# Attention scores on four TensorE tiles, products on two, and block means of v by TensorE, in a kernel of banded attention and two feed-forward networks

## Chip, cores, metric

One NeuronCore of a Trainium2 chip. The metric is the device time of one execution in microseconds (us), as the median of several runs. The engines are PE (TensorE, matmuls, with its weight loads PEld), DVE (VectorE), ACT (ScalarE), POOL (GpSimd) and SP (SyncE, whose queue, SPq, issues all loads and stores here).

## What is computed

Two batches, 8 heads, 768 positions, head size 64. Each query sees the keys less than 16 positions away, and beside them one summary for each block of 32 positions: the maximum of the block's keys and the mean of its values. The result, as 1536 tokens by 512, goes through two feed-forward networks (FFN) with 2048 hidden units.

```python
# attention; block = 32, window = 16
k_sum = k.reshape(B, H, nb, block, D).max(axis=3)
v_sum = v.reshape(B, H, nb, block, D).mean(axis=3)
scores_l = scale * np.matmul(q, k.transpose(0, 1, 3, 2))
mask_l = np.abs(pos[:, None] - pos[None, :]) < window
scores_s = scale * np.einsum('bhsd,bhnd->bhsn', q, k_sum) + np.log(block)
scores_all = np.concatenate([np.where(mask_l, scores_l, -1e9), scores_s], axis=-1)
a = softmax(scores_all)
x = np.matmul(a, np.concatenate([v, v_sum], axis=2))
# then, on x as [tokens, 512]:
h = x @ w_in;  x = (h - np.tanh(h)) @ w_out
h = x @ w_in2; out = (h * np.tanh(softplus(h))) @ w_out2
```

## The kernel before

**Units.** The attention is done in 12 units u, two batches of six windows of 128 queries. Heads are taken in 4 pairs (hp), e = 0 or 1 is the head of a pair, and s = 0 or 1 the half of 64 queries in a window. For each half there are 120 keys: 24 summaries of blocks and 96 keys of the band. The host lays out q and k transposed (the two heads of a pair on partitions 0 to 63 and 64 to 127), v by windows (`vw`), and v transposed once more (`vt`) for its block sums.

**Scores** (`qk`). The q of a u lies in a tile `qz` twice, once for each e, with zeros on the other head's 64 partitions, so that the product over all 128 partitions gives one head's scores. A score has 128 rows of weights and 64 output columns (a column tile for each s); 16 of them make one e.

**Softmax and products.** `softmax` takes mask, maximum and exponential of one e (VectorE, L330, then four ScalarE activations, L335), `norm` divides, `a_trans` transposes (TensorE, L355) and copies to `asb`, and `av` multiplies with v (L369): 16 products for one e, all on the column tile of that e. `x_hi` and `x_lo` split the result into two parts that the FFNs multiply apart.

**Summaries.** `k_sum` (VectorE, L264) takes the block maxima of k of a u, `k_fill` copies those of a whole batch beside the band of each u. `v_sum` adds up the loaded `vtc` (VectorE, or GpSimd by halving adds), `v_trans` turns the sums by TensorE (L294) and copies them, scaled by 1/32, into the v tile `vu[0]`; `v_fill` copies them from there by DMA into the two other v tiles (L303). The three v tiles are reused by the u that follow.

**Order.** The schedule is written by hand: each engine works through its instructions in the order of the program. Ahead of the loop stand the loads of the first batch's own k, of q for u = 0 to 2, one v and three vt. Then step j makes the scores of (u, e) = (j // 2, j % 2), the softmax of the step before, the normalisation three steps back, the transposes five steps back and the products six steps back; the table `todo` adds loads, sums and fills at chosen steps, and its loads go to SP's queue in that order. Between the steps stands the conversion of the FFN's weights (L114 to L137), and at the end of the loop the first steps of the FFN, whose 96 steps follow.

Of the kernel before, what the change touches and what calls it, by code (L numbers as in the profile page):

```python
# [26 lines left out]
def kernel(  # L27
# [17 lines left out]
    nc = tc.nc  # L45
# [133 lines left out]
    def attention(actx):  # L179
# [7 lines left out]
        qz = [kq.tile([128, 2, HP, 128], F32, name=f"qz{n}") for n in range(3)]  # L187
        vu = [con.tile([KA, 2, H, D], F32, name=f"vu{n}") for n in range(3)]
# [4 lines left out]

        def q_zero(n):
            for e in range(2):
                other = qz[n][64 * (1 - e):64 * (1 - e) + 64, e]
                if n < 2:
                    nc.vector.memset(other, 0.0)
                else:
                    nc.scalar.copy(other, qz[0][64 * (1 - e):64 * (1 - e) + 64, e])  # L200

        def constants():
# [20 lines left out]
            k_edges(UPB)  # L223
            tops = top_tiles(2)

        vtc, ksum, vsum = {}, {}, {}
# [20 lines left out]
        def load_q(u):  # L247
            for e in range(2):
                nc.sync.dma_start(out=qz[u % 3][64 * e:64 * e + 64, e], in_=qt_d[u, 64 * e:64 * e + 64])

        def load_v(u):
            for s in range(2):
                nc.sync.dma_start(out=vu[u % 3][WND[s][0]:WND[s][1], s], in_=vw_d[u, s])

        def load_vt(b, g):
            vtc[b, g] = two.tile([128, HP, 256], F32, tag="vtc", name="vtc", bufs=3)
            nc.sync.dma_start(out=vtc[b, g], in_=vt_d[b, g])
# [16 lines left out]
        def v_sum(b, g, part, pool=False):  # L274
            if b not in vsum:
                vsum[b] = two.tile([128, HP, NB], F32, tag="vsum", name="vsum")
            t = vtc[b, g].rearrange("p a (n c) -> p a n c", c=BLK)
            o = vsum[b][:, :, g * 8:(g + 1) * 8]
            t, o = (z[:, 2 * part:2 * part + 2] for z in (t, o))
            if not pool:  # L280
                nc.vector.tensor_reduce(out=o, in_=t, axis=AX.X, op=ALU.add)
                return
            c = BLK // 2
            while c > 1:
                nc.gpsimd.tensor_tensor(
                    out=t[:, :, :, 0:c], in0=t[:, :, :, 0:c], in1=t[:, :, :, c:2 * c], op=ALU.add
                )
                c //= 2
            nc.gpsimd.tensor_tensor(out=o, in0=t[:, :, :, 0], in1=t[:, :, :, 1], op=ALU.add)

        def v_trans(b):
            p = pst("tr")
            for hp in range(HP):
                nc.tensor.transpose(p[0:NB, hp * 128:(hp + 1) * 128], vsum[b][:, hp, :], ident)  # L294
# [6 lines left out]
        def v_fill(n):  # L301
            for s in range(2):
                nc.sync.dma_start(  # L303
                    out=vu[n][SUM[s][0]:SUM[s][1], s], in_=vu[0][SUM[s][0]:SUM[s][1], s]
                )
# [3 lines left out]
        def qk(u, e):  # L309
            p = pst(("s", "tr")[e])  # L310
            pv = p[:, 0:HP * KA].rearrange("p (a n) -> p a n", a=HP)
            for hp in range(HP):
                for s in range(2):
                    k0 = s * (NB + T)
                    nc.tensor.matmul(
                        out=pv[T * s:T * s + T, hp, :],
                        lhsT=qz[u % 3][:, e, hp, T * s:T * s + T],
                        rhs=kt[u % NK][:, hp, k0:k0 + KA],
                    )
            sc[u, e] = pv  # L320
# [43 lines left out]
        def av(u, e):  # L364
            if e == 0:
                xps[u] = pst("x").rearrange("p (a n) -> p a n", a=HP)
            for hp in range(HP):
                for s in range(2):
                    nc.tensor.matmul(  # L369
                        out=xps[u][64 * e:64 * e + 64, hp, T * s:T * s + T],  # L370
                        lhsT=vu[u % 3][:, s, 2 * hp + e, :],
                        rhs=asb[u, e][:, hp, T * s:T * s + T],
                    )
# [27 lines left out]
        for n in range(3):  # L401
            q_zero(n)
# [8 lines left out]
        for u in range(UPB):  # L411
            if u == 0:
                v_sum(0, 0, 1, True)
# [4 lines left out]
        at(1, L(load_v, 1))  # L418
        at(2, L(load_v, 2), L(v_sum, 0, 0, 0))
        at(3, L(load_k, 6), L(load_k, 7), L(v_sum, 0, 1, 1))  # L420
        at(4, L(load_k, 8), L(v_sum, 0, 1, 0), L(v_sum, 0, 2, 0), L(v_sum, 0, 2, 1, True))
        before_av[5] = L(v_trans, 0)
        at(5, L(v_fill, 1), L(v_fill, 2), L(load_k, 9), L(load_k, 10))
# [3 lines left out]
        at(8, L(k_sum, 9), L(load_vt, 1, 0))  # L427
# [338 lines left out]
```

## Time and profile before

| | us |
|---|---|
| runs of the kernel before (3) | 611.49 to 612.99, median 611.64 |
| the profiled execution | 611.33, of which 609.6 span |
| busy: PE, DVE, ACT, POOL | 594.0, 421.1, 330.2, 53.2 |
| first FFN matmul, and the FFN step from which PE no longer stops | 73.46, 94.27 |

A profile shows one execution. Its times count from the start of the span; the 1.7 us between the span and the execution's time lie around it. An engine's idle time is given in square brackets in a timeline, with what ended it. Names such as `s`, `tr`, `aT` and `x` are the four kinds of PSUM tile, each in two copies: the scores of e = 0 are in `s`, those of e = 1 in `tr`, transposes in `aT`, products in `x`; the FFNs use all four.

### The profile page before, as it was taken

How to read it: one execution, taken by the hardware profiler on the slowest of the kernel's cores; microseconds unless marked ns; L12 is line 12 of the kernel's file. 1: busy time of each engine (PE TensorE's matmuls, PEld its weight loads, DVE VectorE, ACT ScalarE, POOL GpSimd, SP SyncE). 2: the span in 40 equal slices, each digit the busy share in tenths (PEclk: the TensorE clock that was granted, in tenths of full speed). 3: DMA queues.
4: the chain of work that ended last, by engine and by line, in shares of the span. 5: the costliest groups of instructions: out<-in, count | busy, mean ns of one | idle time of the engine just before them, and what ended most of it. 6: DMA issues, size and time to landing. Idle time of an engine off the chain costs nothing.

```text
span 609.6 us, 9228 instructions
## 1 busy us (share of the span) xinstructions
PE 594.0 (97%) x3212; PEld 494.0 (81%) x3212; DVE 421.1 (69%) x972; ACT 330.2 (54%) x793; POOL 53.2 (9%) x109
## 2 busy tenths in 40 slices
PE   7698999999999999999999999999999999999997
PEld 6577888888888888888888888888888888888886
DVE  6668967887342222367777579997768777598785
ACT  5678958887242222356776446664454444454442
POOL 5446652000000000000000000000000000000000
PEclk9899999999999999999999999999999999999999
DMA  9999547766121000125662101100010000100001
GB/s 239 232 254 261 162 134 230 230 216 198 45 54 33 1 0 1 34 83 160 198 195 74 52 1 52 53 19 1 1 69 1 1 1 0 70 1 1 1 1 69
DMA packets 32302, 52.20 MB, mean 86 GB/s; under 512 B 3392, under 2 KB 25920, under 8 KB 32256
## 3 DMA queue, kind: packets, MB, share of 16 engines
q1 hardware_dynamic: 32256, 51.62, 29.3%
q8 instruction: 25, 0.41, 0.3%
q14 instruction: 21, 0.17, 0.1%
HBM read 48.07 MB, written 3.15 MB: 84 GB/s over the span
## 4 chain that ended last, share of the span: by engine, by line
PE 90%; DMA 7%; SPq 1%; DVE 1%; POOL 0%; ACT 0%; issue 0%; POOLq 0%
PE s L486 7%; PE aT L486 7%; PE s L487 7%; PE aT L487 7%; PE s L488 7%; PE tr L487 7%; PE x L487 7%; PE aT L488 7%; PE tr L488 7%; PE x L488 7%; PE tr L486 7%; PE x L486 7%; DMA qz<-in_qt_dram 3%; DMA kt<-in_kw_dram 2%; PE x L369 2%; PE aT L355 1%
## 5 line engine op out<-in xcount | busy, mean ns | idle before, releaser
L511 DVE TENSOR_TENSOR glo<-t,ghi 128x512 fp32r<-128x512 f32 x48 | 33.4, 696 | 86.9 <-ACT ghi L506 86.9
L506 ACT ACTIVATE ghi<-t 128x512 fp32r<-128x512 f32 x48 | 30.2, 629 | 97.3 <-PE tr L488 97.3
L486 PE MATMUL s<-xhi,w 128*128 128x512 f32 x192 | 74.9, 390 | 0.0
L486 PE MATMUL aT<-xhi,w 128*128 128x512 f32 x192 | 74.9, 390 | 0.0
L487 PE MATMUL s<-xlo,w 128*128 128x512 f32 x192 | 74.7, 389 | 0.0
L488 PE MATMUL s<-xhi,w 128*128 128x512 f32 x192 | 74.7, 389 | 0.0
L487 PE MATMUL aT<-xlo,w 128*128 128x512 f32 x192 | 74.7, 389 | 0.0
L488 PE MATMUL aT<-xhi,w 128*128 128x512 f32 x192 | 74.7, 389 | 0.0
L114 ACT ACTIVATE top<-raw 128x256 f16<-128x256 bf16 x128 | 61.5, 486 | 12.3 <-ACT w L132 5.3
L121 DVE SCALAR_TENSOR_TENSOR cv<-raw,top 128x256 int32<-128x256 int32 x128 | 55.5, 435 | 11.3 <-ACT top L114 7.7
L132 ACT ACTIVATE w<-cv 128x256 fp32r<-128x256 f32 x120 | 47.6, 402 | 10.7 <-DVE cv L121 9.7
L137 DVE TENSOR_TENSOR w<-cv,w 128x256 fp32r<-128x256 f32 x114 | 48.4, 426 | 0.1
L542 DVE SCALAR_TENSOR_TENSOR t<-n,r 128x512 f32<-128x512 f32 x48 | 33.1, 689 | 17.5 <-ACT r L539 17.3
L335 ACT ACTIVATE aa<-aa,neg 128x120 f32<-128x120 f32 x96 | 36.6, 383 | 15.0 <-DVE neg L330 15.0
L511 DVE TENSOR_TENSOR glo<-n,ghi 128x512 fp32r<-128x512 f32 x48 | 33.1, 690 | 15.3 <-ACT ghi L506 15.3
L506 ACT ACTIVATE ghi<-n 128x512 fp32r<-128x512 f32 x48 | 30.3, 631 | 24.3 <-PE tr L487 16.1
L486 PEld LDWEIGHTS s<-xhi,w 128*128 128x128 f32 x192 | 36.0, 188 | 7.6
L486 PEld LDWEIGHTS aT<-xhi,w 128*128 128x128 f32 x192 | 36.0, 188 | 7.6
L488 PEld LDWEIGHTS s<-xhi,w 128*128 128x128 f32 x192 | 36.1, 188 | 7.5
L488 PEld LDWEIGHTS aT<-xhi,w 128*128 128x128 f32 x192 | 36.1, 188 | 7.5
L487 PEld LDWEIGHTS s<-xlo,w 128*128 128x128 f32 x192 | 36.0, 188 | 7.4
L487 PEld LDWEIGHTS aT<-xlo,w 128*128 128x128 f32 x192 | 36.0, 188 | 7.4
(99 smaller groups left out, 1307.6 us busy)
## 6 DMA issues: line engine op xcount, KB each, us to landing
raw<-in_w_dram SPq DMA_DIRECT2D x128, 255.8 KB, 3.6
vu<-in_vw_dram SPq DMA_DIRECT2D x24, 192.0 KB, 6.0
qz<-in_qt_dram SPq DMA_DIRECT2D x24, 128.0 KB, 6.9
vtc<-in_vt_dram SPq DMA_DIRECT2D x6, 512.0 KB, 6.8
out_dram<-o SPq DMA_DIRECT2D x9, 256.0 KB, 2.1
kt<-in_kw_dram SPq DMA_DIRECT2D x6, 320.0 KB, 6.4
kt<-in_kw_dram SPq DMA_DIRECT2D x6, 256.0 KB, 4.3
out_dram<-t SPq DMA_DIRECT2D x3, 256.0 KB, 2.1
```

The lines of the kernel that those rows point to most:

```text
L114: nc.scalar.activation(out=tops[n % len(tops)].bitcast(F16).rearrange("p (n t) -> p n t", t=2)[:, :, 1], in_=raws[n].bitcast(BF16).rearran ...
L121: nc.vector.scalar_tensor_tensor(out=tmps[n], in0=raws.pop(n).bitcast(I32).rearrange("p (n t) -> p n t", t=2)[:, :, 0], scalar=13, in1=top ...
L132: nc.scalar.activation(out=hi, in_=t, func=ACTF.Copy)
L137: (nc.gpsimd if on_pool else nc.vector).tensor_tensor(out=W[i][:, 1, o:o + PW], in0=tmps.pop(n).bitcast(F32), in1=W[i][:, 0, o:o + PW].bit ...
L335: nc.scalar.activation(out=aa[u][:, e, hp, :], in_=aa[u][:, e, hp, :], func=ACTF.Exp, scale=-1.0, bias=neg[u][:, e, hp:hp + 1], accum_out= ...
L369: nc.tensor.matmul(out=xps[u][64 * e:64 * e + 64, hp, T * s:T * s + T], lhsT=vu[u % 3][:, s, 2 * hp + e, :], rhs=asb[u, e][:, hp, T * s:T ...
L486: nc.tensor.matmul(out=out, lhsT=w[0], rhs=x[0], start=first, stop=False)
L487: nc.tensor.matmul(out=out, lhsT=w[0], rhs=x[1], start=False, stop=False)
L488: nc.tensor.matmul(out=out, lhsT=w[1], rhs=x[0], start=False, stop=last)
L506: nc.scalar.activation(out=ghi, in_=t, func=ACTF.Copy)
L511: nc.vector.tensor_tensor(out=glo, in0=t, in1=ghi.bitcast(F32), op=ALU.subtract)
L542: nc.vector.scalar_tensor_tensor(out=ts[z], in0=ns[z], scalar=2.0, in1=rs[z], op0=ALU.add, op1=ALU.mult)
```

## The change

It does three things.

1. **Scores.** q is loaded once into a tile `qt`, by one DMA in place of two, without zeros. A score uses the 64 partitions of its head as weights' rows. The scores of both e of a u are made at the even step, e in the innermost loop, so that the instructions go round four tiles of 64 x 64.
2. **Products.** `av` makes both e of a u at the odd step, again e innermost, so that the instructions go round two column tiles.
3. **Means of v.** The loads of `vt`, `v_sum` and `v_trans` go. There are seven v tiles instead of three, and all six of the first batch are loaded ahead of the loop. GpSimd writes zeros into the summary rows of the v tiles and builds two constants: `means`, which holds 1/32 at a block's rows, and `fold`, four identities of 24 stacked. At step 4 (and 17 for the second batch) `v_part` multiplies the six v with `means` in 12 products over four column tiles of 32, and ScalarE copies the result to `vp`; at step 5 (18) `v_fold` adds up the four parts and two ScalarE copies write the means into the batch's first v tile; ten DMAs per batch, not four, then fill the other five.

```diff
-        qz = [kq.tile([128, 2, HP, 128], F32, name=f"qz{n}") for n in range(3)]
-        vu = [con.tile([KA, 2, H, D], F32, name=f"vu{n}") for n in range(3)]
+        qt = [kq.tile([128, HP, 128], F32, name=f"qt{n}") for n in range(3)]
+        NV = UPB + 1
+        vu = [con.tile([KA, 2, H, D], F32, name=f"vu{n}") for n in range(NV)]
+        ZC = 4 * (UPB - 1)
+        means = [con.tile([KA, ZC + 32], F32, name=f"means{s}") for s in range(2)]
+        fold = con.tile([128, NB], F32, name="fold")
...
+            for n in range(NV):
+                for s in range(2):
+                    nc.gpsimd.memset(vu[n][SUM[s][0]:SUM[s][1], s], 0.0)
+            for s in range(2):
+                nc.gpsimd.memset(means[s], 0.0)
...
+        def v_part(b):
+            p = pst("aT")
+            for k in range(UPB // 2):
+                for t in range(4):
+                    w, s = 2 * k + t // 2, t % 2
+                    nc.tensor.matmul(
+                        out=p[32 * t:32 * t + 32, :],
+                        lhsT=means[s][:, ZC - 4 * w:ZC - 4 * w + 32],
+                        rhs=vu[(b * UPB + w) % NV][:, s].rearrange("p h d -> p (h d)"),
+                        start=k == 0, stop=k == UPB // 2 - 1,
+                    )
+            vpart[b] = two.tile([128, H * D], F32, tag="vp", name="vp", bufs=1)
+            nc.scalar.activation(out=vpart[b], in_=p, func=ACTF.Copy)
+
+        def v_fold(b):
+            p = pst("aT")
+            nc.tensor.matmul(out=p[0:NB, :], lhsT=fold, rhs=vpart[b])
+            n = b * UPB % NV
             for s in range(2):
                 nc.scalar.activation(
-                    out=vu[0][SUM[s][0]:SUM[s][1], s].rearrange("p h d -> p (h d)"), in_=p[0:NB, :],
-                    func=ACTF.Copy, scale=1.0 / BLK,
+                    out=vu[n][SUM[s][0]:SUM[s][1], s].rearrange("p h d -> p (h d)"), in_=p[0:NB, :],
+                    func=ACTF.Copy,
                 )
...
-        def qk(u, e):
+        def qk(u):
...
             for hp in range(HP):
                 for s in range(2):
-                    k0 = s * (NB + T)
-                    nc.tensor.matmul(
-                        out=pv[T * s:T * s + T, hp, :],
-                        lhsT=qz[u % 3][:, e, hp, T * s:T * s + T],
-                        rhs=kt[u % NK][:, hp, k0:k0 + KA],
-                    )
+                    for e in range(2):
+                        d = slice(64 * e, 64 * e + 64)
+                        k0 = s * (NB + T)
+                        nc.tensor.matmul(
+                            out=sc[u, e][T * s:T * s + T, hp, :],
+                            lhsT=qt[u % 3][d, hp, T * s:T * s + T],
+                            rhs=kt[u % NK][d, hp, k0:k0 + KA],
+                        )
...
         load_q(0)
-        load_vt(0, 0)
+        load_v(0)
+        load_v(1)
         load_q(1)
-        load_v(0)
-        load_vt(0, 1)
+        for u in range(2, UPB):
+            load_v(u)
         load_q(2)
-        load_vt(0, 2)
...
-            at(2 * u + 1, L(load_v, u))
...
+        for u in range(UPB + 1, NU):
+            at(2 * u - 7, L(load_v, u))
...
-        before_av[5] = L(v_trans, 0)
-        at(5, L(v_fill, 1), L(v_fill, 2), L(load_k, 9), L(load_k, 10))
+        before_av[4] = L(v_part, 0)
+        before_av[5] = L(v_fold, 0)
+        at(5, *[L(v_fill, u) for u in range(1, UPB)])
+        at(5, L(load_k, 9), L(load_k, 10), L(load_v, 6))
```

On SP's queue, around the fills of the first batch (numbers in names are those of the tiles: `kt_90`, `kt_91` and `kt_92` hold k of u = 9, 10 and 11 here, `vu_100` is the first v tile), there stands before:

```order
L249 DMA qz_99<-in_qt_dram 64x512 x2
L303 DMA vu_101<-vu_100 24x512 x2
L303 DMA vu_102<-vu_100 24x512 x2
L229 DMA kt_90<-in_kw_dram 128x4x160
L229 DMA kt_91<-in_kw_dram 128x4x160
L253 DMA vu_100<-in_vw_dram 96x512 x2
L249 DMA qz_97<-in_qt_dram 64x512 x2
L229 DMA kt_92<-in_kw_dram 128x4x160
```

Three fills more, two DMAs each, now stand ahead of the k loads of u = 9 and 10, and one v load more ahead of that of u = 11.

On the same queue at the same place after the change:

```order
L263 DMA qt_99<-in_qt_dram 128x512
L313 DMA vu_101<-vu_100 24x512 x2
L313 DMA vu_102<-vu_100 24x512 x2
L313 DMA vu_103<-vu_100 24x512 x2
L313 DMA vu_104<-vu_100 24x512 x2
L313 DMA vu_105<-vu_100 24x512 x2
L244 DMA kt_90<-in_kw_dram 128x4x160
L244 DMA kt_91<-in_kw_dram 128x4x160
L267 DMA vu_106<-in_vw_dram 96x512 x2
L263 DMA qt_97<-in_qt_dram 128x512
L267 DMA vu_100<-in_vw_dram 96x512 x2
L244 DMA kt_92<-in_kw_dram 128x4x160
```

The k loads kept their order among themselves and moved behind the fills as a block.

On TensorE, from the end of the scores of u = 2 (`kt_91`) to the start of those of u = 3 (`kt_92`), there stands before:

```order
L315 MATMUL tr<-kt_91,qz_99 64x120 x8
L355 MATMUL aT<-ident,aa 120x128 x4
L294 MATMUL tr<-ident,vsum 24x128 x4
L315 MATMUL s<-kt_92,qz_97 64x120 x8
```

The four transposes of the sums of v stood between the transposes of a and the next scores.

On TensorE at the same place after the change (a row is one product here, of two instructions; the eight means before the first row read alike):

```order
L291 MATMUL aT<-vu_104,means_107 32x512
L291 MATMUL aT<-vu_104,means_108 32x512
L291 MATMUL aT<-vu_105,means_107 32x512
L291 MATMUL aT<-vu_105,means_108 32x512
L368 MATMUL aT<-ident,aa 120x128 x4
L302 MATMUL aT<-vp,fold 24x512
L329 MATMUL s<-kt_92,qt_97 64x120
L329 MATMUL tr<-kt_92,qt_97 64x120
```

The means stand between the scores of u = 2 and the first transposes of a, the fold behind these, and scores of both e follow in turn.

## Rows read from the trace of the kernel before

**Rows 1.** The page's part 2, busy tenths in 40 slices of the span.

```profile
PE   7698999999999999999999999999999999999997
...
DMA  9999547766121000125662101100010000100001
```

**Rows 2.** Windows by stage: us, busy of PE, PEld, DVE, ACT, POOL, PEclk, DMA, GB/s.

```profile
10.30:17.10 6.80, 3.97 (x65) 3.61 (x66) 5.56 (x37) 4.65 (x24) 4.16 (x10) 1.00 1.06 274
...
40.30:58.43 18.13, 15.69 (x224) 13.35 (x222) 17.61 (x88) 15.43 (x65) 12.57 (x22) 1.00 1.03 257
58.43:73.46 15.03, 15.03 (x216) 12.99 (x217) 13.36 (x64) 13.23 (x58) 7.66 (x13) 1.00 0.59 167
73.46:94.27 20.81, 20.81 (x166) 17.14 (x165) 13.60 (x33) 14.54 (x39) 13.04 (x18) 1.00 0.52 150
```

**Rows 3.** VectorE's timeline: start, us, instruction, idle time before it and its releaser.

```profile
33.74 0.69 DVE L264 TENSOR_REDUCE ksum<-kt 128x16 f32<-128x512 f32 x1 [2.96 <-DMA kt<-in_kw_dram]
...
39.21 0.69 DVE L264 TENSOR_REDUCE ksum<-kt 128x16 f32<-128x512 f32 x1 [1.69 <-DMA kt<-in_kw_dram]
```

**Rows 4.** The page's part 6, DMA issues: count, KB each, us to landing.

```profile
vu<-in_vw_dram SPq DMA_DIRECT2D x24, 192.0 KB, 6.0
qz<-in_qt_dram SPq DMA_DIRECT2D x24, 128.0 KB, 6.9
vtc<-in_vt_dram SPq DMA_DIRECT2D x6, 512.0 KB, 6.8
out_dram<-o SPq DMA_DIRECT2D x9, 256.0 KB, 2.1
kt<-in_kw_dram SPq DMA_DIRECT2D x6, 320.0 KB, 6.4
kt<-in_kw_dram SPq DMA_DIRECT2D x6, 256.0 KB, 4.3
```

**Rows 5.** Windows around the third q, columns as in Rows 2.

```profile
15.00:17.07 2.07, 0.01 (x1) 0.04 (x1) 1.63 (x4) 1.65 (x10) 1.52 (x2) 1.00 1.03 259
...
17.77:21.18 3.41, 3.41 (x30) 2.92 (x25) 2.74 (x15) 2.41 (x15) 1.74 (x4) 0.50 1.04 239
```

**Rows 6.** TensorE's timeline, scores (L315) and half products (L369).

```profile
17.07 1.22 PE L315 MATMUL s<-kt,qz 128*64 128x120 f32 x15 [2.53 <-DMA qz<-in_qt_dram]
...
65.81 0.32 PE L315 MATMUL tr<-kt,qz 128*64 128x120 f32 x1
...
65.92 0.99 PE L315 MATMUL tr<-kt,qz 128*64 128x120 f32 x15
...
72.39 1.15 PE L369 MATMUL x<-asb,vu 120*64 120x64 f32 x16
...
86.32 1.15 PE L369 MATMUL x<-asb,vu 120*64 120x64 f32 x16
```

**Rows 7.** ScalarE from 41.00 to 66.30: busy, mean ns, idle before and releaser.

```profile
L335 ACT ACTIVATE aa<-aa,neg 128x120 f32<-128x120 f32 x40 | 15.2, 383 | 3.4 <-DVE neg L330 3.4
...
L377 ACT ACTIVATE xhi<-x 128x512 fp32r<-128x512 f32 x5 | 2.9, 586 | 0.2 <-PE x L369 0.2
```

**Rows 8.** SP's queue, issues by start and us.

```profile
24.44 3.88 SPq L303 DMA_DIRECT2D vu<-vu  x4
28.42 1.51 SPq L229 DMA_DIRECT2D kt<-in_kw_dram  x2
...
40.35 0.79 SPq L253 DMA_DIRECT2D vu<-in_vw_dram  x2
```

**Rows 9.** Line L303, the fills of v: ns min/median/max of an issue.

```profile
L303 SPq DMA_DIRECT2D vu<-vu x8: 714/748/1192, 24.4 to 62.8; - x8
```

**Rows 10.** VectorE's copy that feeds the products at 72.39.

```profile
70.36 0.68 DVE L359 COPY asb<-aT 120x512 f32<-120x512 f32 x1
```

**Rows 11.** GpSimd's timeline: last constants, and weights' low parts.

```profile
7.62 0.57 POOL L98 MEMSET top<- 128x256 int32 x2
...
91.58 2.56 POOL L137 TENSOR_TENSOR w<-cv,w 128x256 fp32r<-128x256 f32 x3 [1.42 <-ACT w L132]
```

More of the change, by code (lines that the diff above doesn't have):

```diff
@@ L192, in attention @@
         WND = ((NB, KA), (0, KW))
[L194 to L200, printed above, removed]
         def constants():
@@ L223, in constants @@
             k_edges(UPB)
+            for n in range(NV):
[3 more added lines that the diff above has]
+                nc.gpsimd.memset(means[s], 0.0)
+                cols = means[s][:, ZC + 2 * s:ZC + 2 * s + 2]
+                nc.gpsimd.memset(cols, 1.0 / BLK)
+                own = WND[s][0] + WIN
+                for pattern, base, mul in (([[-BLK, 2]], -own, 1), ([[BLK, 2]], own + BLK - 1, -1)):
+                    nc.gpsimd.affine_select(
+                        out=cols, in_=cols, pattern=pattern, base=base, channel_multiplier=mul,
+                        compare_op=ALU.is_ge, fill=0.0,
+                    )
+            nc.gpsimd.tensor_tensor(out=fold, in0=ident[:, 0:NB], in1=ident[:, 32:32 + NB], op=ALU.add)
+            for t in (2, 3):
+                nc.gpsimd.tensor_tensor(out=fold, in0=fold, in1=ident[:, 32 * t:32 * t + NB], op=ALU.add)
             tops = top_tiles(2)
-        vtc, ksum, vsum = {}, {}, {}
+        ksum, vpart = {}, {}
         def load_k(u):
@@ L247, in load_q @@
         def load_q(u):
-            for e in range(2):
-                nc.sync.dma_start(out=qz[u % 3][64 * e:64 * e + 64, e], in_=qt_d[u, 64 * e:64 * e + 64])
+            nc.sync.dma_start(out=qt[u % 3], in_=qt_d[u])
         def load_v(u):
             for s in range(2):
[L253 to L257, printed above, removed]
+                nc.sync.dma_start(out=vu[u % NV][WND[s][0]:WND[s][1], s], in_=vw_d[u, s])
         def k_sum(u):
@@ L272, in k_fill @@
                 eng.tensor_copy(kt[u % NK][:, :, o:o + NB], ksum[u // UPB])
[L274 to L286, printed above, removed]
-                )
-                c //= 2
-            nc.gpsimd.tensor_tensor(out=o, in0=t[:, :, :, 0], in1=t[:, :, :, 1], op=ALU.add)
@@ L312, in qk @@
             for hp in range(HP):
                 for s in range(2):
[L314 to L320 removed]
+                    for e in range(2):
+                        d = slice(64 * e, 64 * e + 64)
[4 more added lines that the diff above has]
+                            rhs=kt[u % NK][d, hp, k0:k0 + KA],
+                        )
@@ L362, in a_trans, with av @@
             asb[u, e] = t
-        def av(u, e):
-            if e == 0:
-                xps[u] = pst("x").rearrange("p (a n) -> p a n", a=HP)
+        def av(u):
+            xps[u] = pst("x").rearrange("p (a n) -> p a n", a=HP)
             for hp in range(HP):
                 for s in range(2):
[L369 to L373, printed above, removed]
+                    for e in range(2):
+                        nc.tensor.matmul(
+                            out=xps[u][64 * e:64 * e + 64, hp, T * s:T * s + T],
+                            lhsT=vu[u % NV][:, s, 2 * hp + e, :],
+                            rhs=asb[u, e][:, hp, T * s:T * s + T],
+                        )
         def x_hi(u):
@@ L426, in attention @@
         at(7, L(k_sum, 8), L(load_k, 11))
-        at(8, L(k_sum, 9), L(load_vt, 1, 0))
-        at(9, L(k_sum, 10), L(load_vt, 1, 1))
+        at(8, L(k_sum, 9))
+        at(9, L(k_sum, 10))
         at(10, L(k_sum, 11), L(k_fill, 6))
-        at(11, L(load_vt, 1, 2), L(v_sum, 1, 0, 0))
-        at(12, L(v_sum, 1, 0, 1, True), L(conv_ahead, n_raw))
-        at(13, L(v_sum, 1, 1, 0))
-        at(14, L(v_sum, 1, 1, 1, True))
-        at(15, L(v_sum, 1, 2, 0, True))
-        at(16, L(v_sum, 1, 2, 1))
-        before_av[17] = L(v_trans, 1)
-        at(17, L(v_fill, 1), L(v_fill, 2))
+        at(15, L(conv_ahead, n_raw))
+        before_av[17] = L(v_part, 1)
+        before_av[18] = L(v_fold, 1)
+        at(18, *[L(v_fill, u) for u in range(7, NU)])
         for u in range(7, 12):
@@ L455, in attention @@
                 x_hi(xu)
-            if j < NJ:
-                qk(j // 2, j % 2)
+            if j < NJ and j % 2 == 0:
+                qk(j // 2)
             nu, nr = divmod(j - 3, 2)
@@ L470, in attention @@
                 before_av[j]()
-            if LA <= j < NJ + LA:
-                av(*divmod(j - LA, 2))
+            if LA <= j < NJ + LA and (j - LA) % 2:
+                av((j - LA) // 2)
             for f in todo.get(j, []):
```

22 lines of the change are left out of this document (6 added, 16 removed).

## Prediction

> **What bounds the kernel now.** I read the page's slices first. TensorE is at 9 in every slice of 15.2 us but the first, the second, the fourth and the last, and the DMA engines are at 9 in just the first four [rows 1]. So there is a front of some 60 to 90 us in which TensorE waits, and behind it a stretch in which TensorE is the bound. The windows by stage say the same [rows 2]: from 58.43 us on PE is busy for the whole of each window, before that it is not. Only the front is touched by the change, so the sum is that of a shift: how much earlier or later does TensorE come to the step that starts at 94.27, from which on it never pauses.
>
> What holds the front is then read from VectorE's timeline [rows 3]. Two of its idle stretches, of 2.96 and 1.69 us, end at a block maximum of k (L264) that waits for a load of k: those of u = 9 and u = 11, at 33.74 and 39.21. The engine works in order, so all softmaxes queued behind stand too. After that VectorE (17.61 of 18.13 us) and ScalarE (15.43) are nearly full up to 58.43 [rows 2].
>
> **What the change does, part by part.**
>
> *Loads before the third q.* Before, q of u = 2 is issued behind six own k loads, two q, two vt and one v; after, behind six k, two q and all six v of the first batch. With the sizes of the page, two issues to a q or a v [rows 4]: up to and with it 6 x 256 + 3 x 256 + 2 x 512 + 384 = 3712 KB before, 6 x 256 + 3 x 256 + 6 x 384 = 4608 KB after. The 896 KB more (0.92 MB) are 3.5 us at the 259 GB/s of that stretch [rows 5]. The scores of u = 2 waited for this q until 17.07 [rows 6]; so they start at 20.6. Over the whole front 3 MB of vt loads go, which helps only where a load ends a wait.
>
> *Scores on four tiles.* Fifteen scores in a row take 0.99 us, one alone 0.32: one starts each (0.99 - 0.32) / 14 = 0.05 us. A half of the products, 16 instructions, takes 1.07 (from 72.39 to the window's end at 73.46), 0.067 each [rows 2, 6]. A score moves 120 columns, a product 64. That the scores are no slower means that their two column tiles already run at once; the products of a half, all on one tile, do not. On four tiles the 32 scores of a u should take 8 x 0.10 = 0.8 us, not 1.6; at half clock, twice that. TensorE stood from before 15.00 until 17.07 and was granted 0.50, its lower level of 1.2 GHz, from 17.77 to 21.18, 4.1 us after its restart [rows 5]. It will stand longer after the change, so I let it run at half clock from 20.6 to 24.7: scores of u = 2 done at 22.3.
>
> *Means on TensorE.* Twelve products of 512 columns, 24 instructions, on four column tiles, 6 each. By 120 columns in 0.10 us, 512 take 0.43: 2.6 us, doubled until 24.7. That makes 2.8 of the 6 passes by 24.7, 1.4 us for the rest and 0.2 to drain: 26.3. ScalarE copies the result (0.59, as the 512-column copy of x in [rows 7]), then does the four exponentials of u = 2 that are queued behind (4 x 0.38), then the first copy of the folded means: 29.0. The fold, 512 columns once, lies beside the exponentials.
>
> *Fills on SP's queue.* Before, four copies of the means into two other v tiles start at 24.44, and the k load of u = 9 is issued behind them at 28.42 [rows 8]. After, there are ten, from 29.0 on. One keeps the queue for 0.748 us in the median [rows 9], about 0.80 with the step to the next: 8.0 us. The load of u = 9 is issued at 37.1, 8.7 later than before. Up to and with k of u = 11 there follow 320 x 3 + 384 x 2 + 256 = 1984 KB (2.03 MB), 7.9 us at 257 GB/s [rows 2], and a start of 1.1 (the 2.1 us of 256 KB out, less its 1.0 at that rate [rows 4]). k of u = 11 lands at 46.1, not 39.21: **+6.9**.
>
> *What is made good behind it.* From 41.00 to 66.30 ScalarE is idle for 3.4 us before exponentials and 0.2 before copies of x [rows 7], while VectorE is nearly full. Three sums of v go from VectorE there, of as many elements as a maximum of k, 0.69 each [rows 3], 2.1 in all; the added copy of the means takes 0.6 of ScalarE. So between 2.1 - 0.6 = 1.5 and 3.6 - 0.6 = 3.0; I take 2.5, as the two then wait for each other less: **-2.5**. From 58.43 to 73.46 VectorE (13.36 of 15.03) and ScalarE (13.23) stay nearly full [rows 2] with the same work as before. TensorE's faster products gain there only its own delay: the copy that feeds the products at 72.39 [rows 6] starts at 70.36 and takes 0.68 [rows 10], so TensorE comes to it 1.35 late: **-1.3**.
>
> *Tail.* From 73.46 on TensorE is the bound, with four half products among its work up to and with 86.32 [rows 6]. Four halves at 1.07 become two whole ones that should take no more each than one half: 2.1 us less, of which I count **-2.0**, since two tiles end a little after one. The last half gains nothing: the first layer at 94.27 needs weights whose low parts GpSimd ends at 94.14 [rows 11], a chain that does not pass through the products.
>
> *At no gain or cost.* The memsets of q go, where VectorE waits for k anyway, and GpSimd's sums of v. Fourteen memsets of 24 x 512 come on GpSimd, 0.57 each by the two of 128 x 256 that take 0.57 [rows 11], 8.0 us; with some 2.3 for the other constants GpSimd comes to its fills of k at about 18.5, before the q of 20.6. Without that cover each us of delay would cost one. The means of the second batch fall where TensorE has idle time.
>
> **Sum.** +6.9 - 2.5 - 1.3 - 2.0 = +1.1 us on the profiled execution's 611.33 us (span 609.6): 612.4. The median of the runs, 611.64, is 0.3 above that execution: 612.7.
>
> **A rule against the products' gain.** The scores of before load weights of all 128 rows on either column tile and still start each 0.05 us [rows 6]: a tile's weights come in while the other tile works. The Trainium skill, TensorE: Matmul & The Clock Gate, Part 3, says that weight loads overlap with running products only where their row groups differ; the new products use the same rows on both tiles. By that rule the 2.0 would be lost; this trace speaks against it.
>
> **Rivals.**
> 1. *The relief of the loads reaches the end (faster).* If ten copies on an otherwise empty queue cost what two v loads do, 0.79 for the pair [rows 8], they take 4.0 us, not 8.0, and k of u = 11 is 4.0 earlier: 608.7. For it: 3 MB less to load, so that queues are emptier. Against: eight such copies, none under 0.714 [rows 9].
> 2. *The four column tiles of the means run one after the other (slower).* 24 x 0.43 = 10.3 us, not 2.6, in the first batch, all ahead of the fills: +7.7, 620.4. It decides as soon as a pass of four takes over 0.6 us. The trace shows two tiles at once, never four.
> 3. *TensorE stays at half clock (slower).* It stands twice for 6 us and more. If the means run wholly at 0.50, they take 5.2 us, not 3.9: +1.3. If, after the wait for k of u = 9, a u at twice its time (0.8 of scores, 1.1 of products, about as much of transposes by my estimate, so twice 3 us) exceeds the pitch at which VectorE feeds it (13.36 us for about three u's in [rows 2], 4.5 each), each of three u's adds up to 1.5, most of it hidden by that pitch's own gaps: 615.
> 4. *The change does not do there what it says: the products on two tiles don't overlap.* The 2.0 us are lost: 614.7.
>
> **How the numbers follow.** The forecast 0.39, rival 1 0.32, rival 2 0.07, rival 3 0.12, rival 4 0.10. About 0.3% (1.8 us) is what a measurement of this kernel can tell from no change. Low end: rival 1 with 3.0 made good (-0.5), loads at the 274 GB/s of [rows 2] (-0.5) and a tail of 3 (-1.0): 606.7. High end: rival 4 with 1.5 made good (+1.0) and part of rival 3: 617. Rival 2 is left outside, with a little at both ends. Within 0.3% lie most of the forecast's spread (609.8 to 613.5) and the near edge of rival 1: 0.38. Faster 0.34, slower 0.28. The likeliest time is 612.7.
>
> **What would show each step.** In the profile of the changed kernel: the scores of u = 2 start at 20 to 21 us behind a q load; the means end near 26; ten copies stand on SP from 29 to 37; VectorE is idle for several us before the maximum of u = 9 and again before that of u = 11 at about 46; ScalarE and VectorE are then full to about 75; the first FFN step starts at 75 to 77, the last pause ends at 95. I am wrong if VectorE doesn't wait there, if the copies take half the time, or if a whole set of products takes the 2.1 us of two halves.

## The result, and the profile after

The changed kernel takes 617.48 us in the median of five runs (616.25 to 618.95), beside 612.68 (five runs) for the kernel before: a ratio of 1.0082, 95% interval 1.0058 to 1.0105. It is slower by 0.8%. The forecast was 612.7, in a range of 606.7 to 617.0, with a chance of 0.28 for slower; the time lies 0.5 us above the range. The profiled execution took 616.25 us (span 614.5), 4.9 more than that of before.

Part 2 of the page of the changed kernel, against [rows 1]:

```profile
PE   5657989999999999999999999999999999999997
...
PEclk8687999999999999999999999999999999999999
DMA  9655556776302000034663101100010000100001
```

TensorE is at 9 from the seventh slice on, not from the fifth, and the DMA engines, which were at 9 in the first four slices, are there in the first alone. So loads are fewer, as meant, but they no longer fill the time. ScalarE's and SP's timelines, and then VectorE's, say what they wait for:

```profile
27.33 0.60 ACT L298 ACTIVATE vp<-aT 128x512 f32<-128x512 f32 x1 [6.85 <-PE aT L291]
```

```profile
29.96 8.40 SPq L313 DMA_DIRECT2D vu<-vu  x10
38.46 1.30 SPq L244 DMA_DIRECT2D kt<-in_kw_dram  x2
...
42.38 0.55 SPq L244 DMA_DIRECT2D kt<-in_kw_dram  x1
```

```profile
41.93 0.69 DVE L274 TENSOR_REDUCE ksum<-kt 128x16 f32<-128x512 f32 x1 [7.38 <-DMA kt<-in_kw_dram]
...
47.60 0.69 DVE L274 TENSOR_REDUCE ksum<-kt 128x16 f32<-128x512 f32 x1 [1.91 <-DMA kt<-in_kw_dram]
...
63.22 0.69 DVE L372 COPY asb<-aT 120x512 f32<-120x512 f32 x1 [1.74 <-PE aT L368]
```

ScalarE waits 6.85 us for the means. The ten fills keep SP's queue from 29.96 to 38.4, where four began at 24.44 [rows 8]; k of u = 9 is issued at 38.46, not 28.42. VectorE's wait for it grew from 2.96 [rows 3] to 7.38 us. The third row is a wait that the kernel before did not have in this place; it is taken up below.

TensorE's timeline, with the scores of u = 2 (21.06), the means, the products of u = 5 (66.68), the scores of u = 9 (67.76) and the first FFN step:

```profile
21.06 0.43 PE L329 MATMUL s<-kt,qt 64*64 64x120 f32 x1 [4.53 <-DMA qt<-in_qt_dram]
...
23.10 4.07 PE L291 MATMUL aT<-vu,means 120*32 120x512 f32 x24
...
66.68 1.15 PE L382 MATMUL x<-asb,vu 120*64 120x64 f32 x32
67.76 0.31 PE L329 MATMUL s<-kt,qt 64*64 64x120 f32 x1
...
68.74 0.65 PE L368 MATMUL aT<-ident,aa 128*120 128x128 f32 x4
...
81.72 0.50 PE L492 MATMUL s<-xhi,w 128*128 128x512 f32 x1
```

A product is two instructions here, and the 16 for one e that are spoken of ahead of the prediction are instructions of eight products. A whole set of products, 32 instructions, takes 1.08 us (66.68 to 67.76), as long as 16 did before, and the 32 instructions of the scores of a u take 0.98 (67.76 to 68.74), where 16 had taken about that [rows 6]. Both parts do on TensorE what the change says.

To see where the time goes, the same instruction is found in two traces by its place among its kind on its engine (the maximum of k of u = 9 is the tenth), and the two starts are subtracted. In us against the kernel before, one profiled execution of each kernel, with the experiments that are told below (E1 to E14 for short):

| start of | before | after | E1 | E3 | E4 | E5 | E11 | E14 |
|---|---|---|---|---|---|---|---|---|
| VectorE, first softmax | 11.68 | +0.0 | +1.7 | -0.5 | +0.8 | +0.1 | +0.1 | -0.3 |
| softmax u = 2, e = 0 | 19.70 | +3.5 | +5.6 | -0.8 | +3.9 | +1.8 | +1.6 | -1.0 |
| maximum of k, u = 9 | 33.74 | +8.2 | +3.1 | -4.1 | +9.2 | -0.4 | -0.4 | -3.8 |
| maximum of k, u = 11 | 39.21 | +8.4 | +3.1 | -4.7 | +10.7 | -0.3 | -0.5 | -4.2 |
| softmax u = 7, e = 1 | 53.49 | +7.1 | +1.8 | -5.4 | +9.4 | -1.5 | -1.2 | -3.4 |
| softmax u = 8, e = 0 | 55.49 | +8.3 | +1.6 | -4.2 | +9.0 | -1.7 | -1.2 | -3.4 |
| softmax u = 9, e = 1 | 64.45 | +9.6 | +2.8 | -4.1 | +13.0 | -0.5 | -1.7 | -3.3 |
| last store's issue (its end) | 606.88 | +5.1 | -1.6 | -8.5 | +13.7 | -4.9 | -6.1 | -4.6 |

Three things stand in the column of after: 8.4 us are lost up to the maximum of u = 11, 1.15 more up to the softmax of u = 9, and 4.4 come back between there and the end. The first row shows how far two executions differ of themselves: the changed kernel and E1 are the same up to there and lie 1.7 us apart, which the other rows carry along.

### The profile page after: what moved, and what is told of

The parts are those of the page before. It is cut to its first block, busy times and chain, and to the rows that moved or that the text cites. A ratio compares the mean times of both kernels' runs of the same rounds, so it can differ in the third digit from the quotient of the medians.

```text
span 614.5 us, 9299 instructions
## 1 busy us (share of the span) xinstructions
PE 585.2 (95%) x3256; PEld 479.5 (78%) x3256; DVE 415.7 (68%) x961; ACT 329.9 (54%) x793; POOL 52.3 (9%) x109
## 4 chain that ended last, share of the span: by engine, by line
PE 90%; DMA 3%; ACT 2%; DVE 2%; SPq 1%; issue 1%; POOL 0%; POOLq 0%
PE s L492 7%; PE aT L492 7%; PE s L494 7%; PE aT L493 7%; PE s L493 7%; PE tr L493 7%; PE x L493 7%; PE aT L494 7%; PE tr L494 7%; PE x L494 7%; PE tr L492 7%; PE x L492 7%; PE x L382 2%; ACT aa L348 1%; DMA kt<-in_kw_dram 1%; PE aT L368 1%
## 5 line engine op out<-in xcount | busy, mean ns | idle before, releaser
L121 DVE SCALAR_TENSOR_TENSOR cv<-raw,top 128x256 int32<-128x256 int32 x128 | 55.4, 434 | 10.7 <-ACT top L114 6.9
L132 ACT ACTIVATE w<-cv 128x256 fp32r<-128x256 f32 x120 | 47.5, 402 | 10.0 <-DVE cv L121 9.0
L512 ACT ACTIVATE ghi<-n 128x512 fp32r<-128x512 f32 x48 | 30.3, 632 | 24.4 <-PE tr L493 16.1
```

The costliest lines, as they stand in the source:

```text
L121: nc.vector.scalar_tensor_tensor(out=tmps[n], in0=raws.pop(n).bitcast(I32).rearrange("p (n t) -> p n t", t=2)[:, :, 0], scalar=13, in1=top ...
L132: nc.scalar.activation(out=hi, in_=t, func=ACTF.Copy)
L512: nc.scalar.activation(out=ghi, in_=t, func=ACTF.Copy)
```

## Experiments

### The two halves of the change, each alone

E3, the kernel before with the new scores and products:

```diff
-                        lhsT=qz[u % 3][:, e, hp, T * s:T * s + T],
-                        rhs=kt[u % NK][:, hp, k0:k0 + KA],
+                            lhsT=qt[u % 3][d, hp, T * s:T * s + T],
+                            rhs=kt[u % NK][d, hp, k0:k0 + KA],
...
-            if LA <= j < NJ + LA:
-                av(*divmod(j - LA, 2))
+            if LA <= j < NJ + LA and (j - LA) % 2:
+                av((j - LA) // 2)
```

> The kernel before with the new scores and the new products alone; vt, sums of v, three v tiles and four fills stay. Theory 1 (the products bring what the tail showed, the loss is all in the means): 606.5 to 608.5, 3 to 4.5 us faster than before. Theory 2 (a TensorE that finishes sooner stands longer and is granted the lower clock, which eats the gain): 610.5 or more.

601.60 us against 611.44, ratio 0.9859 (0.9822 to 0.9897): 9.8 us faster, by far more than either theory gave. It is also faster than both kernels of this study.

E4, the changed kernel with `qz`, `qk` and `av` of before put back:

> The changed kernel with the scores and products of before (q twice with zeros, one e at a time); the means by TensorE, seven v tiles and ten fills stay. Theory 1: the k waits are as in the changed kernel, and without the products' gain the end is at 619 to 622. Theory 2 (the means cost little, scores and products lose the time): 611 to 613.

625.96 against 611.44, ratio 1.0263 (1.0218 to 1.0308): 14.5 us slower, again more than expected. The two medians' differences, -9.8 and +14.5, make +4.7; the change itself measured +4.8. So what is slow is the means, and scores and products pay for two thirds of it.

Where E3's gain arises is told by the two parts of it apart. E11 takes over `av` alone, E14 `qk` and the load of q alone:

> The kernel before with the new products alone; scores, q and the means are those of before. Theory 1 (the 10 us that scores and products bring together come from two places: 4.4 us in the tail from the products, 4 to 5 us before 40 us from the scores and the one DMA for q): nothing changes before 40 us, the tail brings 4.0 to 4.8 us, the end is at 607. Theory 2 (the products bring the early gain too): 602 to 604.

607.26 against 611.32, ratio 0.9938 (0.9906 to 0.9970).

> The kernel before with the new scores and the one DMA for a q alone; products and means are those of before. Theory 1 (scores and q bring the early part of the 10 us): the maximum of u = 11 comes 3.5 to 5 us earlier than in the kernel before, the tail adds nothing, the end is at 606.5 to 608. Theory 2 (scores bring time only together with the products): the maximum of u = 11 and the end stay within 1.5 us of the kernel before.

606.19 against 612.24, ratio 0.9874 (0.9807 to 0.9942). In the table E14 gains its 4.2 us up to the maximum of u = 11 and then keeps them, while E11 has 0.5 there and gains 4.4 behind the softmax of u = 9 (from -1.7 to -6.1). Theory 1 of both holds: the scores and the q load gain in front, the products in the tail (606.19 is 0.3 below what E14's theory gave). How the front gains is read from SP's queue of E3:

```profile
19.40 0.54 SPq L240 DMA_DIRECT2D qt<-in_qt_dram  x1
21.49 3.33 SPq L294 DMA_DIRECT2D vu<-vu  x4
24.93 1.70 SPq L221 DMA_DIRECT2D kt<-in_kw_dram  x2
```

Its fills start 2.95 us before those of [rows 8], and k of u = 9 is issued 3.5 earlier. In the kernel before, the queue came to the fills only at 24.4, with two pairs of q DMAs just ahead:

```profile
20.47 1.36 SPq L249 DMA_DIRECT2D qz<-in_qt_dram  x2
...
23.13 1.22 SPq L249 DMA_DIRECT2D qz<-in_qt_dram  x2
```

A q as one DMA takes 0.54 in E3's row, and E3's queue is free at 19.94 and waits for the means. Most of its lead is older than these rows: it issues k of u = 6 and 7 at 14.89, the kernel before at 17.52. E14 changes the scores and the load of q together, so what each of them brings is not shown. VectorE's waits for k shrink to a quarter and to two thirds of those of [rows 3]:

```profile
29.60 0.69 DVE L255 TENSOR_REDUCE ksum<-kt 128x16 f32<-128x512 f32 x1 [0.69 <-DMA kt<-in_kw_dram]
...
34.53 0.69 DVE L255 TENSOR_REDUCE ksum<-kt 128x16 f32<-128x512 f32 x1 [1.16 <-DMA kt<-in_kw_dram]
```

### The fills ahead of the k loads

E1 moves k of u = 9 and 10 and the v of u = 6 ahead of all fills, and six of the ten fills behind k of u = 11:

```diff
-        at(5, *[L(v_fill, u) for u in range(1, UPB)])
         at(5, L(load_k, 9), L(load_k, 10), L(load_v, 6))
+        at(5, *[L(v_fill, u) for u in range(1, 3)])
...
-        at(7, L(k_sum, 8), L(load_k, 11))
+        at(7, L(k_sum, 8), L(load_k, 11), *[L(v_fill, u) for u in range(3, UPB)])
```

> The changed kernel, but the k loads of u = 9 and 10 and the v load of u = 6 are issued ahead of the fills, and the fills of u = 3 to 5 stand behind the k load of u = 11. Theory 1 (the fills on SP's queue delay k, and the whole front shifts with it): the maximum of u = 9 starts before 36 us instead of 41.93, that of u = 11 before 40 instead of 47.60, and most of those 7 to 9 us reach the end: 607 to 610. Theory 2 (the front is held by ScalarE, VectorE and a slow TensorE clock, the k wait is hidden by them): the maxima come earlier, but the end stays within 1.5 us of 616.3.

609.12 against 611.44, ratio 0.9970 (0.9951 to 0.9988). It is 2.3 us faster than the kernel before where the change was 4.8 slower: 7.1 us, or 8.4 between the two medians, all of it from an order on a queue. SP's queue of E1:

```profile
25.80 2.08 SPq L244 DMA_DIRECT2D kt<-in_kw_dram  x2
...
32.34 3.54 SPq L313 DMA_DIRECT2D vu<-vu  x4
...
38.12 0.62 SPq L244 DMA_DIRECT2D kt<-in_kw_dram  x1
```

VectorE no longer waits for k of u = 9, and for u = 11 only 1.16 us:

```profile
42.27 0.69 DVE L274 TENSOR_REDUCE ksum<-kt 128x16 f32<-128x512 f32 x1 [1.16 <-DMA kt<-in_kw_dram]
```

Theory 1 holds (609.1 for 607 to 610), with maxima 0.8 and 2.3 us later than it said; this execution was 1.7 late from its first softmax on.

E10 leaves the order and takes away six of the ten fills, to tell their number from their late start:

> The changed kernel with the fills of u = 3 to 5 and 9 to 11 left out, so four DMAs for a batch and not ten; the summary rows of those v stay zero. Theory 1 (each fill holds SP's queue for 0.84 us, and the k loads behind): k of u = 9 is issued 5.0 us earlier, its maximum starts at about 37 instead of 41.93, and 4 to 5 us of it reach the end: 612.5. Theory 2 (the late start of the fills is what counts, their number is covered by the DMA engines' own backlog): 616.5.

615.69 against 611.32, ratio 1.0053 (1.0028 to 1.0077). SP's queue, and VectorE's two maxima:

```profile
31.71 3.45 SPq L313 DMA_DIRECT2D vu<-vu  x4
35.25 1.99 SPq L244 DMA_DIRECT2D kt<-in_kw_dram  x2
...
39.87 0.55 SPq L244 DMA_DIRECT2D kt<-in_kw_dram  x1
```

```profile
39.13 0.69 DVE L274 TENSOR_REDUCE ksum<-kt 128x16 f32<-128x512 f32 x1 [2.83 <-DMA kt<-in_kw_dram]
...
46.79 0.69 DVE L274 TENSOR_REDUCE ksum<-kt 128x16 f32<-128x512 f32 x1 [3.88 <-DMA kt<-in_kw_dram]
```

Four fills take 3.45 us for 8.40 with ten: the price was right. k of u = 9 gains nearly what it should, 2.8 us in an execution whose fills began 1.75 later. But the wait for u = 11 doubled, 6.9 us after its issue instead of 5.2, so at 46.79 nearly all is lost again. Theory 1 fails for the end: six fills less are worth 0.4 us, each kernel set against its own runs of before, or 1.8 between the medians. What counts, by E1 beside it, is that loads stand behind the means at all: the changed kernel issues no load from 23.54 to 38.46 us, E10 none from 24.97 to 35.25. In E10 the DMA engines do nothing from 28 to 32 us, and from 40 on they are full (the last two columns, as in [rows 2]):

```profile
28.00:30.00 2.00, 1.78 (x17) 0.55 (x10) 0.46 (x1) 0.92 (x4) 0.00 (x0) 1.00 0.00 0
...
40.00:42.00 2.00, 1.13 (x28) 0.73 (x18) 1.97 (x12) 1.95 (x9) 0.89 (x1) 1.00 1.04 244
```

Why k of u = 11 took 6.9 us is open.

E2 loads q of u = 2 ahead of four of the v:

```diff
+        load_q(2)
         for u in range(2, UPB):
             load_v(u)
-        load_q(2)
```

> The changed kernel, but q of u = 2 is loaded ahead of the v of u = 2 to 5. Theory 1 (the late q of u = 2 costs only through the means and the fills behind them): the scores of u = 2 start at 16 to 18 us instead of 21.06, the fills still not before 28, the end moves by less than 1.5 us. Theory 2 (the late q itself is passed on): the end comes 3 to 3.5 us earlier, 613.

615.40 against 611.44, ratio 1.0081 (1.0052 to 1.0110). That is 4.0 us slower than before where the change was 4.8: moving the q is worth about 1 us (2.1 between the medians), nearer to theory 1. But the scores of u = 2 came at 18.87 and not at 16 to 18, and no longer waited for q:

```profile
18.87 0.46 PE L329 MATMUL s<-kt,qt 64*64 64x120 f32 x1 [1.07 <-POOL kt L282]
```

What they wait for is GpSimd's fill of k, which stands behind the 7.97 us of zeros for the v tiles. The prediction had seen that delay and counted on the late q to cover it; with q early it becomes the limit, and E2 doesn't price the q alone. E5 makes both moves:

> The changed kernel with both moves: k of u = 9 and 10 ahead of the fills, and q of u = 2 ahead of the v of u = 2 to 5. Theory 1 (ScalarE's copy of the partial means, which waits for the last v, stands ahead of the exponentials of u = 2 and limits what the earlier q brings): 1 to 2 us faster than with the k loads moved alone, 607 to 608. Theory 2 (the late q holds the front by itself): 3.5 us faster than that, 605.5.

605.85 against 612.16, ratio 0.9910 (0.9877 to 0.9942): 3.3 us before E1, as theory 2 said. In the profiled executions 1.6 of that is E1's later start (first row of the table), so the share of the q may be as little as 1.7, which would be theory 1's figure; but with the k loads ahead of the fills the q does count. Here too the scores of u = 2 wait for GpSimd and not for q, for 3.66 us:

```profile
19.37 0.46 PE L329 MATMUL s<-kt,qt 64*64 64x120 f32 x1 [3.66 <-POOL kt L282]
```

No run with the means goes without these zeros, so what that would bring is not shown. E12 adds one step: `v_part` at step 5 and `v_fold` at step 6.

> The changed kernel with the k loads ahead of the fills, q of u = 2 ahead of the v of u = 2 to 5, and the means of the first batch one step later, so that ScalarE's copy of the partial means stands behind the first exponentials of u = 2. Theory 1 (ScalarE's wait for the means held those exponentials for some 4 us): they start right behind their maximum at about 21 us, and the end is 1.5 to 4 us before the 605.9 of the run without this step. Theory 2 (the k loads come no earlier, so the gain stays in the front): within 1 us of 605.9.

606.79 against 611.32, ratio 0.9910 (0.9879 to 0.9941): nothing beyond E5. The exponentials of u = 2 did come 5.4 us earlier than in E5 (from 26.7 to 21.3), but the time was lost again at the next load, on VectorE:

```profile
39.96 0.69 DVE L274 TENSOR_REDUCE ksum<-kt 128x16 f32<-128x512 f32 x1 [4.82 <-DMA kt<-in_kw_dram]
```

k of u = 11 is issued behind four fills that wait for the means, in E12 as in E5. Theory 2 holds.

In E8 the same order, k ahead of fills, was given to E3:

> The kernel before with the new scores and products alone, and with the k loads of u = 9 and 10 ahead of the four fills. VectorE there still waited 0.69 us for k of u = 9 and 1.16 for k of u = 11. Theory 1 (the fills hold the k loads in this kernel too, and the end follows): the wait for u = 9 goes, the end comes 0.5 to 1.8 us earlier than 601.6. Theory 2 (the loads are limited by the DMA engines, not by the queue): within 0.4 us of 601.6.

604.15 (601.09 to 606.01) against 612.16, ratio 0.9877 (0.9837 to 0.9918); beside E3's 601.60 this is no gain, and the spread is too wide to call it a loss. In its profiled execution the front did gain, as theory 1 said: the maxima of u = 9 and 11 start 1.7 and 1.0 us before E3's, without a wait. The gain went again before the softmax of u = 9, where VectorE waits 3.44 us (at 56.53) for transposes that TensorE makes behind a wait of 1.95 for a q, with the granted clock at 0.50 from 53.2 to 56.6; E3 waits 1.63 there. So this run does not settle what the order is worth in that kernel.

### The 1.15 us lost behind the loads

In the table the 1.15 are a gain of 1.3 up to the softmax of u = 7 and two losses: 1.2 before the softmax of u = 8, and 1.2 before that of u = 9.

*The lower clock.* VectorE's wait of 1.74 us at 63.22 ends at a transpose by TensorE. TensorE's windows around it:

```profile
45.10:53.06 7.96, 7.06 (x76) 5.80 (x76) 5.99 (x31) 5.79 (x25) 2.67 (x3) 0.50 0.85 245
53.06:59.04 5.98, 3.76 (x75) 3.04 (x75) 5.61 (x33) 5.37 (x24) 1.93 (x2) 1.00 0.46 135
59.04:63.30 4.26, 4.26 (x68) 3.84 (x69) 2.52 (x13) 3.93 (x18) 1.37 (x1) 0.60 0.42 125
```

TensorE stood from 39.4 to 45.1 and again, 2.2 us, before 59.04. In the window behind the first the granted clock is at 0.50, the level of 1.2 GHz; in that behind the second it is at 0.60 in the mean, so at the lower level for most of it. E6 fills the second stretch with extra products:

```diff
             xps[u] = pst("x").rearrange("p (a n) -> p a n", a=HP)
+            if u == 4:
+                for n in range(18):
+                    nc.tensor.matmul(out=xps[u][:, 0, :], lhsT=ident, rhs=ident, start=n == 0, stop=n == 17)
```

> The changed kernel with 18 extra products of 128 columns ahead of the products of u = 4, in the idle stretch of TensorE before 59.04 us; their result is overwritten. Theory 1 (the lower clock of 59.9 to 63.3 us is what adds 1.2 us between the scores and the softmax of u = 8): the clock stays at its upper level there, the softmax of u = 8 comes 1.2 us earlier against that of u = 7, the end 1 to 1.3 us earlier, 616.2 in the median. Theory 2 (the clock is hidden there): the end stays at 617.5.

617.77, ratio 1.0105 (1.0073 to 1.0136). The clock stayed up (1.00 from 52.6 us on), and the softmax of u = 8 was no earlier. But the test had spoiled itself: its 18 products of two instructions took 4.18 us, so that the true ones started at 60.43 instead of 59.04.

```profile
56.32 4.18 PE L381 MATMUL x<-ident 128*128 128x128 f32 x36
60.43 1.15 PE L385 MATMUL x<-asb,vu 120*64 120x64 f32 x32
```

E9 has nine of them:

> As the run with 18 extra products, but with nine, since the 18 took 4.2 us and held the products back by 1.2 us; nine fit into the 2.2 us in which TensorE stood. Theory 1 (the lower clock at 59.9 to 63.3 us costs 1.2 us): the clock stays at its upper level, the softmax of u = 8 comes 1.0 to 1.3 us earlier against that of u = 7 than in the changed kernel, and most of it is still there at the end. Theory 2 (the wait for the other engines hides the clock): the distance from u = 7 to u = 8 stays within 0.3 us.

618.93, ratio 1.0114 (1.0081 to 1.0146), and inconclusive: in its profiled execution, with k of u = 11 3.5 us later, the lower clock reached from 44.5 to 61.5 and ended ahead of the nine products (61.94). These then held the true ones back to 64.04, and VectorE waited 1.23 us at the upper clock. E13 fills both stretches:

```diff
             p = pst("aT")
+            if (u, e) == (2, 0):
+                for n in range(22):
+                    nc.tensor.matmul(out=p[:, 0:128], lhsT=ident, rhs=ident, start=n == 0, stop=n == 21)
```

> The changed kernel with 22 extra products of 128 columns ahead of the transposes of u = 2, e = 0, so in the stretch from 39.4 to 45.1 us in which TensorE stands, and nine ahead of the products of u = 4; their results are overwritten. Theory 1 (TensorE's lower clock, which follows these two stretches, makes the 1.2 us between the softmax of u = 7 and that of u = 8): the clock stays at its upper level from about 27 us on, the distance from the second softmax of u = 7 to the first of u = 8 is 2.0 us or less instead of 3.2, the end comes 1 to 1.5 us earlier than the changed kernel's. Theory 2 (something else of the changed kernel makes it): the distance stays at 2.8 us or more with the upper clock.

Its windows there, and VectorE at the place of the row at 63.22:

```profile
54.73:61.51 6.78, 5.79 (x94) 5.11 (x92) 6.51 (x39) 5.71 (x27) 2.09 (x3) 1.00 0.43 136
61.51:65.19 3.68, 3.47 (x73) 2.87 (x72) 3.26 (x15) 3.68 (x17) 1.37 (x1) 1.00 0.19 58
```

```profile
64.79 0.69 DVE L375 COPY asb<-aT 120x512 f32<-120x512 f32 x1 [0.31 <-PE aT L371]
65.40 0.27 DVE L343 CUSTOM_DVE_ANT_0 aa<-s,mask 128x120 f32<-128x120 f32 x1
```

With the upper clock the wait is 0.31 us, not 1.74, and the distance from the softmax of u = 7 to that of u = 8 is 1.80, not 3.23. The clock did not stay up all the way (it was lower before 54.73), but at the disputed place it was. That the clock makes the difference is seen from the work between, first in the changed kernel, then in E13:

```profile
59.04 1.29 PE L382 MATMUL x<-asb,vu 120*64 120x64 f32 x30 [2.22 <-ACT asb L374]
...
62.07 1.67 PE L368 MATMUL aT<-ident,aa 128*120 128x128 f32 x8
```

```profile
62.05 1.15 PE L388 MATMUL x<-asb,vu 120*64 120x64 f32 x30 [0.21 <-ACT asb L377]
...
64.11 1.09 PE L371 MATMUL aT<-ident,aa 128*120 128x128 f32 x8
```

In both these products start 1.55 us before the second softmax of u = 7 (at 60.59 and 63.60). From there to the end of VectorE's wait, over the same products, scores and transposes, it is 4.18 us in one and 2.74 in the other, and these 1.44 are the whole difference of the two distances. Theory 1 holds there. The other kernels agree: the distance is 2.8 to 3.3 us where the lower clock lies on it (after, E2, E3, E8, E10) and 1.4 to 2.0 where it does not (before, E1, E4, E5, E7, E11, E12, E14); E6 and E9 have 3.3 and 2.7 at the upper clock, since their extra products held the true ones back. What brings the lower clock to this place is open. Of the runs without extra products, it is there only in some with both the new scores and the new products; E3, with VectorE's waits for k at 0.69 and 1.16 us, has it, and E1, where TensorE stands 2.21 us at the same place, has not. The end did not follow E13: 618.14, ratio 1.0089 (1.0050 to 1.0127). In this execution k of u = 11 was awaited until 50.62, 3.0 us later than in the changed kernel's; of these 1.6 are left at the end. So the lower clock is 1.2 to 1.4 us of the profiled execution, and no median shows that its removal pays.

*The means of the second batch.* E7 leaves the 24 instructions out:

> The changed kernel without the partial means of the second batch: its 24 instructions on TensorE and the copy of their result are left out, and the fold takes the first batch's partial means. Theory 1 (these instructions stand on TensorE's path at 64 to 66.7 us): x_hi of u = 5 comes 0.9 us earlier against its softmax, the end 0.9 to 1.5 us earlier, 616.2. Theory 2 (they lie where TensorE waits anyway): the end stays at 617.5.

616.37 (614.02 to 618.73), ratio 1.0076 (1.0042 to 1.0109), which cannot be told from the changed kernel's. In the trace, in which k of u = 11 came 3.1 us later, x_hi of u = 5 comes 2.1 us earlier against the second softmax of u = 8, more than theory 1 said; but then TensorE has the lower clock in its first FFN step, which no other kernel but E9 has, and 1.6 of it is lost there:

```profile
81.47:84.88 3.41, 3.41 (x10) 2.67 (x9) 3.15 (x14) 3.41 (x15) 2.29 (x4) 0.50 0.51 180
```

Two of its five runs took 614.0 and 614.2 us, with a mean granted clock of 0.980, and the other three, the profiled one among them, 616.4 to 618.7, with 0.971; whether the two lacked this stretch is not shown.

What the kernels show together: from the second softmax of u = 8 to x_hi of u = 5 it is 0.8 us in those without means on TensorE (before, E3, E8, E11, E14) and 1.8 in those with them and the new scores (after, E1, E2, E5, E6, E9, E12, E13; 2.1 in E10). In E4, whose scores take twice as long, it is 3.2.

## Why the prediction was wrong

**What bounds the kernel.** Right. The time moved with the front, through VectorE's waits for k, and the FFNs behind took what they took before: 512.6 us from the step at 94.27 (99.36 after) to the end.

**Loads before the third q, scores on four tiles, means.** Right: scores of u = 2 at 21.06 for 20.6, at the lower clock; the means behind them from 23.10, in 4.07 us for some 4. GpSimd came to its fills of k at 18.55 for 18.5, so the late q did cover them. At the upper clock the second batch's take 2.72 (63.96 to 66.68) for 2.6, so four column tiles do run at once (one after the other had been put at 10.3), and rival 2 is out.

**Fills.** Right in mechanism, short by 1.5: fills from 29.96 (29.0), 8.40 us (8.0), k of u = 9 issued at 38.46 (37.1), the maximum of u = 11 at 47.60 (46.1). +8.4 for the forecast +6.9; 1.0 of the 1.5 is the later start, 0.4 the price of a fill, 0.84 for 0.80.

**Made good behind it: the step that failed.** The forecast was -2.5, measured is +1.15. The argument was that VectorE, which looks nearly full [rows 2], and ScalarE get shorter by the work that goes. 1.3 came back up to the softmax of u = 7, near the lower bound of 1.5, and as much in E4, with the means alone. What was not in the sum is what TensorE adds there: 1.2 by the lower clock, and 0.95 by the means of the second batch with 0.3 behind them, which had been put at nothing "where TensorE has idle time". TensorE's idle time there is not spare: a transpose that comes later makes VectorE wait. These prices are read from traces; taking the clock (E13) or the means of the second batch (E7) away did not move the median clear of the changed kernel's. Rival 3 had the clock, with some 2.3 us in all and a chance of 0.12, though by another way, the pitch of the u's; it should have been a term.

**Products.** Right that they overlap, so rival 4 is out; short by 1.1. From the softmax of u = 9 to the end 4.4 us came back for 1.3 + 2.0. The first FFN step is 8.26 later (81.72 for 73.46), 1.3 better, as forecast. Behind it 3.1 came back, not 2.0. The prediction counted four half products up to and with 86.32; there are five, at 76.85, 81.35, 83.01, 84.67 and 86.32, and a sixth at 90.34, the last half, which it let gain nothing. After the change three whole sets stand there, at 88.33, 90.73 and 95.43, and three times 1.07 is 3.2. The last half gains too: the step at 94.27 was taken to wait for weights that GpSimd ends at 94.14 [rows 11]. After the change it starts before that work ends:

```profile
99.36 0.39 PE L492 MATMUL s<-xhi,w 128*128 128x512 f32 x1
```

```profile
97.92 2.56 POOL L137 TENSOR_TENSOR w<-cv,w 128x256 fp32r<-128x256 f32 x3 [1.41 <-ACT w L132]
```

So the step does not need the end of that work, and the two ends in the kernel before had only fallen together. The Trainium skill's rule, TensorE: Matmul & The Clock Gate, Part 3, by which weight loads on the same rows would not have overlapped, does not hold here: 32 instructions of 64 columns, all on the same rows, take 1.08 us on two column tiles, as long as 16 on one.

**The scores' own gain.** The prediction gave none to scores and q loads in the front. Alone they bring 4.2 us up to the maximum of u = 11 (E14). In the changed kernel they show as E4's +10.7 against its +8.4, so only 2.3 of them remain. In both the means stand on TensorE right behind the scores of u = 2, and these wait for the q that is loaded behind all six v (until 21.06, and 21.64 in E4), which the scores cannot change.

**Sum.** +8.4 + 1.15 - 4.4 = +5.1 at the last instruction, for a forecast of +1.1: 1.5 from the fills, 3.65 from what was to be made good, less 1.1 from the products. Rival 1, the faster one with 0.32, is refuted: ten fills took 8.40 us, not 4.0. A faster kernel was near all the same: with the queue in another order (E5) the same work takes 605.85.

## What to carry to other kernels

A load that depends on nothing should not stand on an in-order queue behind a copy that waits for a computation: here that order alone was 7 to 8 us, while in E8, where the copies waited for little, it brought nothing that could be measured. When a step is timed as hidden in an engine's idle time, look who waits for the engine's next instruction, and price that chain at the lower clock too. A delay that another wait covers, as GpSimd's zeros here, comes out as soon as that wait is mended. And take a change of several parts apart before it is accepted or dropped: one half of this one is 9.8 us faster than the kernel before.

## What was not expected of the hardware

A load of q as one DMA for 128 rows took 0.35 and 0.54 us of SP's queue (at 17.91 and 19.40 in E3) where two for 64 rows took 1.36 and 1.22 (before, at 20.47 and 23.13): at the same bytes the number of DMAs is paid on the queue. It is not the whole price, since one at 28.75 in E3 took 1.29.

Executions of the same front differ in when one load lands: the maximum of u = 11 starts at 47.5 to 47.6 us in the changed kernel and in E6, and at 50.6 to 51.1 in E7, E9 and E13, all with the same loads in the same order; that of u = 9 starts in all five between 41.7 and 44.0. The cause is open.
